# Column means of w1 in two halves, and a list that hands out PSUM's places

## The chip, the core and the metric

The kernel runs on one core of one Trainium2 chip. The metric is the device time of one execution in microseconds (us). The kernel before takes 205.06 us, the median of three runs (204.96 to 205.13). A core has a matrix engine (PE, whose weight loads are listed apart as PEld), a vector engine (DVE), an activation engine (ACT), a general engine (POOL) and a queue engine (SP) that mostly issues transfers. PE writes its results to PSUM, a small memory of eight banks; DVE and ACT read them from there. The large on-chip memory is SBUF.

## The reference, cut to what matters

One sequence of 2048 tokens with 512 channels goes through a long convolution and then through a two-layer network:

```
h  = x + LN(x) * (irfft(rfft(kv) * rfft(ssm_k)) + kv * ssm_D)   # kv = (short conv of k) * v
h2 = h + relu(LN(h) @ w1) @ w2                                   # w1: 512 x 1376, w2: 1376 x 512
```

The kernel does not apply the mean of the second normalisation to the tokens. Subtracting the mean of h over its 512 channels and then multiplying by w1 is the same as multiplying h by a w1 from whose every column its mean over the 512 rows has been taken. So the means of w1's 1376 columns are computed once, w1 is centered in place, and the scale of the normalisation is applied after the second product. The change concerns this piece of work: when the means are taken, and which PSUM tiles they lie in.

## The kernel before, in words

The program is written in one order by hand (a manual schedule): each engine carries out its instructions in the order in which the code emits them, and only waits for other engines where data or a buffer asks for it. Its stages are:

1. 0 to 48 us: tables, the short convolution, and the first stage of the transform of kernel and sequence (`stage1`).
2. 48 to 82 us: the product stage. Eight rounds of six units each (`pairs`, called u, and `sums`, called us). For each unit PE fills one PSUM tile (`u`, `us`), ACT copies one half of it to SBUF (`copy_k`, L449), and DVE multiplies the other half by that copy (`times`, L501). The u units write their products into `BK`, the us units into `BXs`, a part of the tile `BX`. The last units of the last round end with the products `=s1` (into `BXs`), `=u3` and `=u2` (into `BK`), in this order.
3. 82 to 83.5 us: the column means. POOL has added up the four row blocks of w1 in SBUF (`add_chunks`, into `wsum`, which lies in the tile `st`); four matmuls against a matrix of ones (L533, 344 columns each) add up the partitions. They go to two PSUM tiles, both named `pm`. ACT copies the second of them to SBUF (L633); DVE subtracts the means from w1 in four steps (`center`, L596), the first two from PSUM, the last two from the copy.
4. 83.5 to 106.8 us: the first inverse stage (`inv1`, L610), 16 blocks of four groups. Each group is one matmul of 256 columns that reads `BXs` and two of 128 columns that read `BK`. For the first two blocks the `BXs` matmuls are emitted ahead (`inv1_begin`), four for each block, and the `BK` matmuls follow. ACT or DVE copies each finished block to `ax`, two instructions a block (L278 on ACT, L280 on DVE). The last two blocks are cut into two and four tiles so that their copies end early.
5. 106.6 us: two matmuls of zeros (`fill`, L157) stand in PE's order while the last copies end.
6. 107.4 to 115.1 us: the second inverse stage for the first two of four token quarters (`inv2`, L701, 32 matmuls each). The first writes PSUM's upper four banks (`psZ0`), the second the lower four (`psZ`). After the first, DVE multiplies the result by the normalised x and adds x (`gate`, L687 and L688), which gives the input of the network for that quarter.
7. To the end: for each quarter the network's two layers (`mlp1` L713, `mlp2` L729), with the second inverse stage of the last two quarters and the gates in between.

PSUM's eight banks are one pool of four places of two banks each until the first inverse stage is over: `bank2` takes a tile from it, and the pool decides which place it gets. Before the last round's end every place has been used many times, so each new tile waits for the engine that read the former tile in the same place last. In the built program the column means' first tile lies in the place of the unit u1 of the last round, the second in that of s1; the first block of the inverse stage lies in that of u3, the second in that of u2, the third in that of the second means' tile (which ACT copies), the fourth in that of the first means' tile (which DVE reads in `center`).

Other work stands beside this: SP loads x for the first quarter after the product stage (`load_x`) and transposes it (`lift`), DVE takes the normalisation's statistics behind `center` (`ln1_stats`, then `ln1_norm` after block 3), and POOL prepares angles (`ec_turns`).

Of the kernel before, what the change touches and what calls it, by code (L numbers as in the profile page):

```python
# [9 lines left out]
ALU = mybir.AluOpType  # L10
BF16 = mybir.dt.bfloat16
F32 = mybir.dt.float32
F32R = mybir.dt.float32r
I32 = mybir.dt.int32
PSUM = bass.MemoryType.PSUM
P = 128
# [40 lines left out]
def kernel(  # L57
# [13 lines left out]
    nc = tc.nc  # L71
    _, S, D = A_q.shape
    DFF = B_w1.shape[1]
# [3 lines left out]
    DC = D // P  # L77
# [5 lines left out]
    pl = _Pools(tc)  # L83
# [6 lines left out]
    turnp = pl.push("turnp")  # L90
    early = pl.push("early", side="right")
    kp = pl.push("kp", side="right")
    psum = pl.push("psF", bufs=4, space=PSUM)

# [51 lines left out]
        nc.scalar.activation(out=out, in_=turns, func=ACT.Sin, scale=(-TURN if neg else TURN) / M,  # L148
                             bias=(pbias if neg else nbias)[:])

    def bank2(name):
        return psum.tile([P, 2, 512], F32, tag="ps", name=name)[:]

    def fill(ps, n):

        for _ in range(n):
            nc.tensor.matmul(out=ps, lhsT=zero[:], rhs=zero[:].unsqueeze(1).to_broadcast([P, 4, P]), start=True, stop=True, skip_group_check=True)  # L157
# [110 lines left out]
    def ec_wrap(q):  # L268
        nc.vector.tensor_single_scalar(out=ecw[q], in_=ecw[q], scalar=8191, op=ALU.bitwise_and)
# [85 lines left out]
    ones = consts.tile([P, P], F32R, name="ones")  # L355
# [66 lines left out]
    BXt = bxp.tile([P, 32, 66, DC * 2], F32R, tag="X", name="BX")  # L422
# [14 lines left out]
    wsum = stf[:, 0:DFF]  # L437
# [14 lines left out]

    def pairs(k1):

        ps = bank2("u")
        begun = []

        def do(what):
            x = "KX".index(what[0])
            for i in range(2):  # L460
                t = st[:, k1, 64:192] if i == 0 else st[:, k1, 0:128]
                for dp, pq in enumerate(halves):
                    nc.tensor.matmul(out=ps[:, dp, 256 * x:256 * x + 256], lhsT=t[pq], rhs=cols((BK, BX)[x], pq, k1, i),  # L463
                                     start=not begun, stop=(i == 1), tile_position=(64 * dp, 0), skip_group_check=True)
                begun.append(i)
        return do, ps, "ktu", BK[:, :, :, k1, :]

    def sums(k1):

        ps = bank2("us")  # L470
        begun = []
        ways = {}

        def do(what):
            x, way = "KX".index(what[0]), int(what[1])
            last = {}
            for i in range(2):
                for dp, pq in enumerate(halves):
                    k = k1 + (dp + way - 1) % 2
                    if i == 0 and dp == 0 and (3 - way, dp) in ways:  # L480

                        turn = nc.tensor.nop()
                        for d in range(2):
                            tc.add_manual_dep(turn.ins, ways[3 - way, d], mybir.DependencyInfo(mybir.DependencyClass.Sync, mybir.DependencyReason.DATA))
                    mm = nc.tensor.matmul(out=ps[:, k % 2, 256 * x:256 * x + 256], lhsT=smc[pq, k // 4 % 3, i, k % 4, :],  # L485
                                     rhs=cols((BK, BX)[x], pq, k, i), start=not begun, stop=(i == 1 and what in begun),
                                     tile_position=(64 * dp, 0), skip_group_check=True)
                    last[dp] = mm.ins.name
                begun.extend((what[0] + "12"[2 - way], i))
            for dp in range(2):  # L490
                ways[way, dp] = last[dp]
        return do, ps, "kts", BXs[:, :, k1:k1 + 2, :].rearrange("p g k x -> p k g x")
# [5 lines left out]
    def times(unit, kt=None):  # L498
        do, ps, tag, o = unit
        kt = copy_k(unit) if kt is None else kt  # L500
        nc.vector.tensor_tensor(out=o, in0=ps[:, :, 256:512].rearrange("p b (g x) -> p b g x", x=8),  # L501
                                in1=kt[:].rearrange("p b (g x) -> p b g x", x=8), op=ALU.mult)

# [2 lines left out]
    for c in range(8):  # L508
        units, early = {}, {}
        for step in (OTHER if c else FIRST).split():  # L510
# [6 lines left out]
            u = step[:2]  # L517
# [5 lines left out]
        if c in (2, 4, 5):  # L523
            add_chunks(max(c - 3, 0))

    FS = 344
    cen = {}

    def column_means(ns):
        ps = bank2("pm")  # L530
        for b, n in enumerate(ns):
            cen[n] = ps[:, b, 0:FS]
            nc.tensor.matmul(out=cen[n], lhsT=ones[:], rhs=wsum[:, n * FS:(n + 1) * FS], start=True, stop=True)  # L533
        return ps[:, :, 0:FS]

    column_means((0, 1))
    pm23 = column_means((2, 3))
    pl.pop("skp")
    pl.pop("stp")
    pl.pop("prod")  # L540
# [22 lines left out]
    qT = [late.tile([P, 4, DC, P], BF16, name="qT0")[:]] + [None] * 3  # L563
# [28 lines left out]
        rows_T(qT[q], src)  # L592

    def center(n):
        fs = slice(n * FS, (n + 1) * FS)
        nc.vector.tensor_tensor(out=w1[:, :, fs], in0=w1[:, :, fs],  # L596
                                in1=cen[n].unsqueeze(1).to_broadcast([P, DC, FS]), op=ALU.subtract)

    ax1 = late.tile([P, 32, 2, P], F32R, name="ax1")
    ax = (BX[:, 1].rearrange("p n k x -> p n (k x)").rearrange("p n (m c) -> p n m c", m=2), ax1[:])  # L600
# [28 lines left out]
                     blocks[b][:, 0:n].rearrange("p i d a n -> p a n (i d)")[:, rho].rearrange("p (n m) c -> p n m c", m=2))  # L629

    lift(0)
    later = qT[0].rearrange("p i r t -> p (i r t)").bitcast(F32)[:, 0:2 * FS].rearrange("p (n f) -> p n f", n=2)
    nc.scalar.copy(out=later, in_=pm23)  # L633
    cen[2], cen[3] = later[:, 0], later[:, 1]
    inv1_begin(0)
    inv1_begin(1)

# [3 lines left out]
    for b in range(16):  # L641
        inv1(b, "ADAD" if b == 15 else "AD" if b == 14 else "D" if b in (7, 9, 11, 13) else "A")
        if b == 0:
            for n in range(4):
                center(n)
            ec_wrap(1)
            ln1_stats(0)
        if b == 3:
            ln1_norm(0)
        if b in (8, 9, 10, 11):  # L650
            ec_sins(1, (b - 8,))
        if b == 11:
            load_x(1)
    fill(bank2("psz")[:, 0, :], 2)
    M = bkp.tile([P, 32768], BF16, tag="K", name="M")
    top = [0]

# [28 lines left out]
    def gate(q):  # L686
        nc.vector.tensor_tensor(out=flat(qT[q]), in0=pzs[q][:].rearrange("p i r a n -> p (i r a n)"), in1=flat(qT[q]), op=ALU.mult)  # L687
        nc.vector.tensor_tensor(out=flat(xT[q]), in0=flat(qT[q]), in1=flat(xT[q]), op=ALU.add)  # L688
        hT[q] = xT[q]
        nc.sync.dma_start_transpose(out=xh[q].rearrange("p i (r c) -> p (i r) c", r=DC),  # L690
                                    in_=hT[q].rearrange("p i r t -> p (i r) t"))

    def inv2(q, pool):
        pz = pool.tile([P, 4, DC, 4, 32], F32, tag="pz", name="pz")
        pzs[q] = pz
        for j in range(16):
            i, a = j // 4, j % 4
            w = min(2, 4 - a)
            n2 = 16 * a + 4 * q + i
            for rho in range(2):  # L700
                nc.tensor.matmul(out=pz[:, i, :, a:a + w, :].rearrange("p (s r) a n -> p s r (a n)", s=2),  # L701
                                 lhsT=ax[rho][:, n2 // 2, n2 % 2, :],
                                 rhs=ecore[q][:, rho, i, :, :, 32 * a:32 * a + 32 * w],
                                 start=(rho == 0), stop=(rho == 1), skip_group_check=True)
# [30 lines left out]
            if hook is not None:  # L735
                hook(i)

    pl.pop("psF")
    psz = pl.push("psZ", space=PSUM)
    psz0 = pl.push("psZ0", space=PSUM)  # L740
    ec_turns(2)
    inv2(0, psz0)
    gate(0)
    inv2(1, psz)
    pl.pop("psZ0")
# [68 lines left out]
```

## Time and profile before

| view | value |
|---|---|
| time, median of 3 runs | 205.06 us (204.96 to 205.13) |
| profiled execution: its own time | 205.23 us |
| its span, first to last instruction | 203.1 us |
| outside the span | 2.1 us |
| PE busy | 194.7 us, 96% of the span |
| DVE, ACT, POOL busy | 140.3, 115.1, 79.3 us |
| matmul `pm` (L533) | 4 of 344 columns, 0.32 to 0.43 us each, 82.43 to 83.52 us |
| `center` (L596) | 4 of 1.58 us, 83.99 to 90.07 us |
| copy of the second means (L633) | 0.74 us at 84.19 us |
| mean granted clock of PE | 0.997 |

A PE at 96% says that the chain of work runs through PE nearly everywhere, not that each of its instructions is as short as it could be: matmuls overlap, so the distance from one to the next (here mostly 0.12 us) is what counts, not the duration of one (0.28 us for 256 columns). Time is lost or won where PE stands still or where an instruction leaves PE's queue. Times below are microseconds from the start of the span.

### The profile page before, as it was taken

The numbers are of one execution on the slowest core, as the hardware profiler recorded it, in microseconds if no ns is written. First come the engines' busy times: TensorE is split into PE (matmuls) and PEld (weight loads), VectorE is DVE, ScalarE is ACT, GpSimd is POOL, SyncE is SP. The second block draws the span as 40 slices with busy tenths as digits, with TensorE's granted clock in tenths as the row PEclk, the third lists the DMA queues.
The fourth block names the chain that finished last, engine by engine and source line by source line (L and its number), as shares of the span: only waits on it lengthen the run. The fifth ranks groups of instructions, "written<-read, shape, count | busy, mean of one in ns | idle before, by whom it ended". The sixth has DMA issues, their size and how long they took to land.

```text
span 203.1 us, 4751 instructions
## 1 busy us (share of the span) xinstructions
PE 194.7 (96%) x1929; PEld 136.9 (67%) x1929; DVE 140.3 (69%) x252; ACT 115.1 (57%) x198; POOL 79.3 (39%) x127
## 2 busy tenths in 40 slices
PE   8899899999999999999999999999999999999991
PEld 2565556988899999899998744475445744444460
DVE  4999988796899989997561968994298560360130
ACT  4986785898688777685980188206930174036200
POOL 7979998960569994302003032062002200002000
PEclk9999999999999999999999999999999999999998
DMA  5999990003400000151736999999734705110011
GB/s 190 330 181 226 170 163 3 3 5 91 190 3 0 3 3 0 46 135 29 107 102 203 183 210 213 177 154 94 88 65 97 138 13 103 35 57 14 0 52 52
DMA packets 47300, 19.94 MB, mean 98 GB/s; under 512 B 42186, under 2 KB 45744, under 8 KB 47280
## 3 DMA queue, kind: packets, MB, share of 16 engines
q1 hardware_dynamic: 43616, 16.14, 41.9%
q10 hardware_dynamic: 3664, 3.51, 6.0%
q8 instruction: 15, 0.25, 0.6%
q14 instruction: 5, 0.04, 0.1%
HBM read 7.02 MB, written 2.10 MB: 45 GB/s over the span
## 4 chain that ended last, share of the span: by engine, by line
PE 73%; DVE 1%; ACT 0%; issue 0%
PE ps1m L713 19%; PE ps2m L729 19%; PE psi L610 11%; PE us L485 9%; PE pz L701 7%; PE u L463 7%; PE pm L533 1%; DVE BX L280 0%; DVE BX L501 0%; ACT kts L449 0%; DVE M L731 0%; DVE ax L280 0%
## 5 line engine op out<-in xcount | busy, mean ns | idle before, releaser
L715 ACT ACTIVATE M<-ps1m 128x512 bf16<-128x512 f32 (+1 forms) x44 | 25.1, 595 | 49.4 <-PE ps1m L713 39.0
L729 PE MATMUL ps2m<-M 128*128 128x512 bf16 (+3 forms) x187 | 38.7, 366 | 0.0
L729 PEld LDWEIGHTS <-M 128*128 128x128 bf16 (+1 forms) x187 | 18.2, 98 | 19.9
L713 PEld LDWEIGHTS <-w 128*128 128x128 bf16 (+1 forms) x176 | 17.4, 100 | 19.9
L572 POOL TENSOR_SCALAR rstd<-mv 128x4 f32<-128x4 f32 x8 | 2.2, 276 | 70.2 <-DVE mv L570 70.2
L409 POOL TENSOR_TENSOR smc<-st 64x256 fp32r<-64x256 f32 x32 | 22.8, 731 | 11.2 <-PE us L485 10.3
L731 DVE SCALAR_TENSOR_TENSOR M<-ps2m,rstd,M 128x512 bf16<-128x512 f32 (+1 forms) x13 | 9.2, 707 | 24.2 <-PE ps2m L729 15.7
L501 DVE TENSOR_TENSOR BK<-u,ktu 128x512 fp32r<-128x512 f32 x32 | 21.2, 685 | 3.8 <-ACT ktu L449 3.5
L610 PE MATMUL psi<-inv,BK 128*128 128x128 f32 x128 | 21.1, 255 | 0.0
L449 ACT COPY ktu<-u 128x512 f32<-128x512 f32 x32 | 18.1, 600 | 5.3 <-PE u L463 4.4
L610 PE MATMUL psi<-inv,BX 128*128 128x256 f32 x64 | 20.5, 338 | 0.0
L610 PEld LDWEIGHTS psi<-inv,BK 128*128 128x128 f32 x128 | 19.7, 197 | 0.0
L713 PE MATMUL ps1m<-M,w 128*128 128x512 bf16 (+1 forms) x88 | 19.3, 379 | 0.0
L713 PE MATMUL ps1m<-xT,w 128*128 128x512 bf16 (+1 forms) x88 | 19.3, 379 | 0.0
L485 PE MATMUL us<-BK,smc 64*128 64x256 f32 x128 | 14.4, 300 | 0.4 <-DVE BX L280 0.4
L463 PE MATMUL u<-BK,st 64*128 64x256 f32 x128 | 13.6, 290 | 0.3 <-DVE BX L501 0.2
L485 PE MATMUL us<-BX,smc 64*128 64x256 f32 x128 | 13.3, 281 | 0.0
L463 PE MATMUL u<-BX,st 64*128 64x256 f32 x128 | 13.1, 283 | 0.0
L278 ACT CAST BK<-ps 128x512 fp32r<-128x512 f32 x16 | 9.1, 587 | 6.4 <-PE ps L312 4.4
L610 PEld LDWEIGHTS psi<-inv,BX 128*128 128x128 f32 x64 | 12.1, 196 | 0.3 <-DVE BK L501 0.3
L568 DVE BATCH_NORM_STATS2 st<-M 128x6 f32<-128x512 bf16 x20 | 12.3, 677 | 0.0
L687 DVE TENSOR_TENSOR qT<-pz,qT 128x2048 bf16<-128x2048 f32 x2 | 4.6, 2290 | 10.6 <-DMA qT<-M 6.5
(132 smaller groups left out, 411.6 us busy)
## 6 DMA issues: line engine op xcount, KB each, us to landing
E<-in_A_ssm_k_dram SPq DMA_DIRECT2D x1, 2048.0 KB
out_dram<-M ACTq DMA_DIRECT2D x15, 128.0 KB
w<-in_B_w_dram SPq DMA_DIRECT2D x1, 1376.0 KB
M<-in_B_w_dram ACTq DMA_DIRECT2D x1, 1280.0 KB
M<-in_A_q_dram SPq DMA_DIRECT2D x8, 128.0 KB
xh<-in_A_q_dram SPq DMA_DIRECT2D x4, 128.0 KB
xr<-in_A_q_dram SPq DMA_DIRECT2D x4, 128.0 KB
out_dram<-M ACTq DMA_DIRECT2D x2, 64.0 KB
```

The source lines that it names most:

```text
L409: nc.gpsimd.tensor_tensor(out=smc[pq, c % 3, i, :, 64 * dp:64 * dp + 64], in0=st[pq, ks, 64:128].bitcast(F32), in1=st[pq, ks, 0:64].bitcas ...
L449: nc.scalar.copy(out=kt[:], in_=ps)
L463: nc.tensor.matmul(out=ps[:, dp, 256 * x:256 * x + 256], lhsT=t[pq], rhs=cols((BK, BX)[x], pq, k1, i), start=not begun, stop=(i == 1), til ...
L485: mm = nc.tensor.matmul(out=ps[:, k % 2, 256 * x:256 * x + 256], lhsT=smc[pq, k // 4 % 3, i, k % 4, :], rhs=cols((BK, BX)[x], pq, k, i), s ...
L501: nc.vector.tensor_tensor(out=o, in0=ps[:, :, 256:512].rearrange("p b (g x) -> p b g x", x=8), in1=kt[:].rearrange("p b (g x) -> p b g x", ...
L568: nc.vector.bn_stats(out=st[:, i, :], in_=src[:, i, :])
L610: nc.tensor.matmul(out=o if part == 0 else o[:, P * part - P:P * part], lhsT=src[:, g // 2, :, g % 2::2].rearrange("p c r -> p (c r)"), rh ...
L701: nc.tensor.matmul(out=pz[:, i, :, a:a + w, :].rearrange("p (s r) a n -> p s r (a n)", s=2), lhsT=ax[rho][:, n2 // 2, n2 % 2, :], rhs=ecor ...
L713: nc.tensor.matmul(out=ps1[:fsz, :].rearrange("p (i t) -> p i t", i=4), lhsT=w1[:, c, fc * P:fc * P + fsz], rhs=hT[sc][:, :, c, :], start= ...
L715: nc.scalar.activation(out=h1T[:fsz, fc, :], in_=ps1[:fsz, :], func=ACT.Relu)
L729: nc.tensor.matmul(out=ps2, lhsT=h1T[:ksz, fc, i * P:(i + 1) * P], rhs=w2[:ksz, fc, d0:d0 + w], start=(fc == 0), stop=(fc == NFC - 1))
L731: nc.vector.scalar_tensor_tensor(out=o[:, d0:d0 + w], in0=ps2, scalar=rstd2[:, t, :], in1=xh[sc][:, i, d0:d0 + w], op0=ALU.mult, op1=ALU.add)
```

## The change

The column means are split in three parts of 512, 352 and 512 columns (`THIRDS`) in place of four of 344. The first two are taken where all four were, into the two banks of one `pm` tile, and both are subtracted by DVE from PSUM after block 0. For the third part ACT copies the 512 sums, not the means, from `wsum` to two free columns (k = 32 and 33) of the tile `BX`; this copy replaces that of the second `pm` tile. Behind the first inverse stage one matmul takes the third part's means from there (512 columns in groups of 16, tile `pm2`), in place of one of the two matmuls of zeros. DVE subtracts them (`center(2)`) between `inv2(0)` and `gate(0)` in its order.

The pool of four places becomes four pools of one place, and `bank2` takes the first place of a list. A place goes to the list's end at once, except for the units of the product stage and for `pm`, which are put back when their last reader has been emitted (`leave`). `pm2` must lie in one of the two lower places, since `inv2(0)` writes the upper banks.

In the built program the places of all tiles up to the last product are, but for their numbers, those of before. Behind it, `pm` lies in the place of u1; the first block of the inverse stage in that of s1, the second in that of u3, the third in that of u2, the fourth in that of the first block, the fifth in that of the second, and the sixth in that of `pm`. So the first `BXs` matmul waits for the product `=s1`, the fifth for `=u3`, and the first `BK` matmul for `=u2`. The order on all engines is otherwise that of before.

```
-    psum = pl.push("psF", bufs=4, space=PSUM)
+    psum = [pl.push(f"psF{i}", bufs=1, space=PSUM) for i in range(4)]
+    places = list(range(4))
+    held = {}
...
-    def bank2(name):
-        return psum.tile([P, 2, 512], F32, tag="ps", name=name)[:]
+    def bank2(name, hold=False, at=None):
+        at = places[0] if at is None else at
+        places.remove(at)
+        ps = psum[at].tile([P, 2, 512], F32, tag="ps", name=name)[:]
+        if hold:
+            held[id(ps)] = at, ps
+        else:
+            places.append(at)
+        return ps
+
+    def leave(ps):
+        places.append(held.pop(id(ps))[0])
...
-        ps = bank2("u")
+        ps = bank2("u", True)
...
-        ps = bank2("us")
+        ps = bank2("us", True)
...
                                 in1=kt[:].rearrange("p b (g x) -> p b g x", x=8), op=ALU.mult)
+        leave(ps)
...
-    FS = 344
+    THIRDS = ((0, 512), (512, 864), (864, DFF))
     cen = {}
-    def column_means(ns):
-        ps = bank2("pm")
-        for b, n in enumerate(ns):
-            cen[n] = ps[:, b, 0:FS]
-            nc.tensor.matmul(out=cen[n], lhsT=ones[:], rhs=wsum[:, n * FS:(n + 1) * FS], start=True, stop=True)
-        return ps[:, :, 0:FS]
-
-    column_means((0, 1))
-    pm23 = column_means((2, 3))
+    def column_means(ps, n, sums):
+        cen[n] = ps[:, 0:THIRDS[n][1] - THIRDS[n][0]]
+        nc.tensor.matmul(out=cen[n] if n < 2 else cen[n].rearrange("p (g x) -> p g x", x=16), lhsT=ones[:], rhs=sums, start=True, stop=True)
+
+    pm = bank2("pm", True)
+    for n in range(2):
+        column_means(pm[:, n], n, wsum[:, slice(*THIRDS[n])])
+    wlast = BXt[:, :, 32:34, :].rearrange("p g k x -> p g (k x)")
+    nc.scalar.copy(out=wlast, in_=wsum[:, slice(*THIRDS[2])].bitcast(F32).rearrange("p (g x) -> p g x", x=16))
...
-        fs = slice(n * FS, (n + 1) * FS)
+        fs = slice(*THIRDS[n])
...
-    later = qT[0].rearrange("p i r t -> p (i r t)").bitcast(F32)[:, 0:2 * FS].rearrange("p (n f) -> p n f", n=2)
-    nc.scalar.copy(out=later, in_=pm23)
-    cen[2], cen[3] = later[:, 0], later[:, 1]
...
         if b == 0:
-            for n in range(4):
+            for n in range(2):
                 center(n)
+            leave(pm)
...
-    fill(bank2("psz")[:, 0, :], 2)
+    pm2 = bank2("pm2", at=[p for p in places if p < 2][0])
+    column_means(pm2[:, 0], 2, wlast)
+    fill(pm2[:, 1], 1)
...
-    pl.pop("psF")
+    for i in (3, 2, 1, 0):
+        pl.pop(f"psF{i}")
...
     inv2(0, psz0)
+    center(2)
     gate(0)
```

More of the change, by code (lines that the diff above doesn't have):

```diff
@@ L594, in center @@
     def center(n):
-        fs = slice(n * FS, (n + 1) * FS)
+        fs = slice(*THIRDS[n])
         nc.vector.tensor_tensor(out=w1[:, :, fs], in0=w1[:, :, fs],
-                                in1=cen[n].unsqueeze(1).to_broadcast([P, DC, FS]), op=ALU.subtract)
+                                in1=cen[n].unsqueeze(1).to_broadcast([P, DC, fs.stop - fs.start]), op=ALU.subtract)
     ax1 = late.tile([P, 32, 2, P], F32R, name="ax1")
```

## The prediction

> **What bounds the kernel now.** I read the busy shares first, then the chain of waits in order of time, then the waits of PE, and last the timeline of the two places that the change touches. The page gives PE as the bound, and its chain holds no long wait:
>
> ```profile
> PE 194.7 (96%) x1929; PEld 136.9 (67%) x1929; DVE 140.3 (69%) x252; ACT 115.1 (57%) x198; POOL 79.3 (39%) x127
> ...
> PE 73%; DVE 1%; ACT 0%; issue 0%
> ```
>
> The chain in order of time (start, length, what) shows the two joints, 82.48 to 83.53 and 106.76 to 107.42. What PE saves there moves everything behind it, unless another wait holds it back:
>
> ```profile
> 82.48 1.04 PE pm L533 x4
> 83.52 0.01 issue
> 83.53 23.22 PE psi L610 x192
> 106.76 0.02 issue
> 106.78 0.29 DVE BX L280
> 107.07 0.21 DVE ax L280
> 107.28 0.14 issue
> 107.42 7.65 PE pz L701 x64
> 115.06 0.01 issue
> 115.07 9.66 PE ps1m L713 x44
> ```
>
> The timeline of the first joint (start, length, engine, line, what, in brackets the idle time and its releaser) shows that the joint is not only PE's work:
>
> ```profile
> 82.20 0.68 DVE L501 TENSOR_TENSOR BX<-us,kts 128x512 fp32r<-128x512 f32 x1
> ...
> 82.80 1.28 DVE L501 TENSOR_TENSOR BK<-u,ktu 128x512 fp32r<-128x512 f32 x2
> ...
> 82.94 0.30 PEld L533 LDWEIGHTS pm<-st,ones 128*128 128x128 f32 x2 [0.23 <-DVE BX L501]
> 83.53 1.16 PEld L610 LDWEIGHTS psi<-inv,BX 128*128 128x128 f32 x8 [0.30 <-DVE BK L501]
> ...
> 84.61 1.97 PEld L610 LDWEIGHTS psi<-inv,BK 128*128 128x128 f32 x16
> ```
>
> DVE's last three products end at 82.88, 83.48 and 84.08. PE's queue starts three times right behind them: the second pair of means at 82.94 (0.06 later; its place is that of s1), the first block of the inverse stage at 83.53 (place of u3), the second block at 84.13 (place of u2). A finer look at the weight loads shows the last:
>
> ```profile
> 83.89 0.20 PEld L610 LDWEIGHTS psi<-inv,BX 128*128 128x128 f32 x1
> ...
> 84.13 0.19 PEld L610 LDWEIGHTS psi<-inv,BX 128*128 128x128 f32 x1
> ```
>
> The loads follow each other by 0.12, but between the fourth (83.89) and the fifth (84.13) lie 0.24. So PE follows DVE here, and behind DVE's end at 84.08 stand the second block's four BX matmuls (84.13 to 84.61) before the first BK matmul at 84.61. The inverse stage then runs without a wait.
>
> The second joint and what follows:
>
> ```profile
> 106.58 0.61 PE L157 MATMUL psz<-zero 128*128 128x512 bf16 x2
> ...
> 106.99 0.28 DVE L280 CAST ax<-psi 128x128 fp32r<-128x128 f32 x1
> ```
>
> PE is idle here but for zeros: it waits for the copy that ends at 107.27 and loads weights again at 107.38. Of the 0.80 from 106.58 to 107.38 the zeros take two distances of 0.23 (106.58, 106.81).
>
> **The first joint, step by step.** Before: means until 82.94 (first pair), a wait, second pair, a wait until 83.53, four BX, a wait until 84.13, four BX, BK at 84.61. After, with the same DVE products (nothing ahead of them moves, as the places up to there are the same):
> - Two means matmuls from 82.41, as now: their place is u1's, free now as then. The two first of now were 0.24 apart (82.43, 82.67); the 864 columns at 0.24 to 0.26 for 344 take 0.60 to 0.65, at most until 83.06.
> - The first block waits for 82.88 (s1's product) and starts at 82.94 to 83.06; four BX at 0.12 end at 83.42 to 83.54.
> - The second block waits for 83.48 (u3's place): 83.53; four BX until 84.01.
> - The first BK matmul waits for the last product, 84.08: 84.13, not 84.61.
>
> So the gain is 84.61 − 84.13 = **0.48 us**, the four BX matmuls that now stand behind the last product. Of the 512 columns fewer (0.36 to 0.39) nothing adds to it: the wait for DVE is the end of the path either way. No less than 0.42 either, if the renewed start costs another 0.06.
>
> A price for the new wait: queued behind that BK matmul is the whole inverse stage, and it starts at 84.13 in any case, when the old order started the second block.
>
> **Places in the inverse stage.** Only three places turn at first. The fourth block waits for ACT's two copies of the first block: these end at 86.88 now, the fourth block starts at 87.93 (block 3 begins at 86.50, each takes 1.43), so 1.05 are left, and both move by 0.48. The fifth has 87.87 against 89.36. The sixth waits for DVE's `center(1)`: centering costs 1.58 for 344 columns, so 2.35 and 1.62 for 512 and 352, from 83.99 to 87.96; the block starts at 90.8 − 0.5 = 90.3. All three hidden; without that cover each would cost its lateness.
>
> **ACT's copy of sums.** 128x512 from SBUF, not in the trace. From below 0.59 (a cast of 128x512), from above 0.74 (128x688, the copy that it replaces); I take 0.6. It starts at 83.11, behind ACT's last copy, and ends at 83.7; ACT's next work is block 1's cast at 85.81 − 0.48. Hidden by 1.6. What waits for it (POOL's `mhalf`, SP's load of x) starts at 84.22 now, behind DVE's 84.08, and stays there. SP's later transfers follow the copies and gates and move with them; DVE's statistics come 2.1 earlier (87.96 for 90.07), as x has landed by 88.40, when SP transposes it; none is on the path.
>
> **The second joint.** `pm2` replaces one zero matmul (0.23). 512 columns of this type are not in the trace: from below 0.24 (two of `inv2`'s 256 columns at 0.12), from above 0.63 (the longest means matmul, 0.425, by 512/344). I take 0.39, the 0.26 between means matmuls by 512/344, being the same operands. With the zero matmul 0.62 of 0.80: hidden, 0.18 to spare; at the upper end 0.86, so 0.06 late.
>
> **Center(2).** 2.35 on DVE from its last copy (106.79 after the shift) or `pm2`'s end, at most until 109.3. DVE then waits: now it is idle for 4.15 until `gate(0)` at 111.42, 110.94 after the shift. `inv2(1)`, which waits for `center(2)`, loads weights at 111.10 now, 110.62 then. 1.3 to spare. If the cover were gone it would count fully: `mlp1(0)` loads weights at 115.04, just 0.07 behind the gate's end (113.74 + 1.23), so a late gate moves the path at once.
>
> POOL's angles (106.82 to 109.02) run beside it. The `center` steps that ran beside such angles (84.28 to 86.48) took 1.577 and 1.581, those without 1.583 and 1.587, so I charge nothing. [...]
>
> **Sum.** 0 − 0.48 + 0 + 0 = −0.48 (bounds −0.48 and −0.36, with 0.06 from a renewed start and 0.06 from `pm2`). The profiled execution: 205.23 − 0.48 = 204.75, span 202.6. It stands 0.17 above the median, so against 205.06 the time is **204.58 us**. About 0.2%, 0.41 us, is what a measurement of this kernel can tell from no change, and the gain is near that.
>
> **Rivals.**
> [...]
> - *The gain is given back.* The earlier stage meets something that doesn't move, a transfer or ACT's copies, and waits. **205.06**, within 0.2%. For it: `mlp1(0)` already follows DVE's gate by 0.07. Against: that gate is released by PE (idle 4.15, released by `pz`), and every issue behind 84 us is too.
> - *Slower: center(2) holds gate(0).* Its place is ahead of the gate in DVE's order. It decides from 110.94 on: it must take over 4.1, not 2.35, to delay the gate, and over 5.0 to make the kernel slower by 0.2% (0.48 + 0.41 more). Twice its price plus 0.4 for a late start, 5.1, would give 110.94 + 1.0 for the gate, so **205.6**. Against it: all four steps lie between 1.577 and 1.587.
> - *The list does not change the wait.* If the first block still had u3's place, the four BX would stay behind the last product: 0, **205.06**. The built order excludes this, and it goes with the second rival.
>
> **How the numbers follow.** Forecast 0.76 (its own range 204.35 to 204.75: 0.48, less up to 0.12, with 0.1 for the spread of runs and as much again for a joint that closes tighter); late joint 0.06; given back 0.11; slower 0.07. The predicted time is the forecast's, 204.58. Four fifths of the forecast lie beyond 0.41, so faster 0.61; the rest with the second and third case makes within 0.2% 0.32; slower 0.07. The range reaches from 204.3 to 205.1, over the late joint and the gain given back; outside stay the slower case and little else.
>
> **What would show it.** In the profile after: weight loads of `psi` at about 82.95, 83.53, and the first BK at 84.13, with DVE's last product still ending at 84.08; `pm` of two matmuls; block casts on ACT 0.48 earlier, with ACT still waiting for PE; `pm2` starting at about 106.1 and the first `pz` load at 106.9, still released by a copy; `center(2)` of 2.35 ending before 109.4, with DVE idle ahead of the gate; PE without a wait from there on; a span of 202.6. The prediction is wrong if the first BK load is not at 84.13, if `pz` is released by PE itself, or if the gate starts without DVE idle ahead of it.

## The result, and the profile after

The changed kernel takes 204.27 us (median of 8 runs, 203.94 to 204.74), the kernel before 205.13 us beside it (8 runs, 204.91 to 205.31). The ratio is 0.9955, with a 95% interval of 0.9937 to 0.9974: it is faster by 0.45%. The forecast was 204.58 us and a gain of 0.48; the gain is 0.86 us, and the time lies 0.03 us below the range.

The profiled execution of the changed kernel took 204.07 us, with a span of 202.3. The page gives nearly the same shares by engine as before:

```profile
PE 73%; DVE 1%; issue 0%; ACT 0%
```

The chain of waits of the changed kernel (start, length, what) around the two joints:

```profile
82.23 0.59 PE pm L547 x2
82.81 23.18 PE psi L626 x192
...
106.01 0.29 DVE BX L293
106.31 0.21 DVE ax L293
106.51 0.14 issue
106.65 7.64 PE pz L717 x64
```

Of the 1.04 us of means 0.59 are left, and the inverse stage follows them without a gap. From its start on the chain has the lengths of before: 23.18 (23.22), the same wait for the last copy, 7.64 (7.65). The timeline of the first joint (start, length, engine, line, what, idle time and releaser) shows what became of the three starts behind VectorE's (DVE's) products:

```profile
82.18 0.63 PE L547 MATMUL pm<-st,ones 128*128 128x512 f32 x2
82.55 1.28 DVE L514 TENSOR_TENSOR BK<-u,ktu 128x512 fp32r<-128x512 f32 x2
82.69 1.15 PEld L626 LDWEIGHTS psi<-inv,BX 128*128 128x128 f32 x8 [0.23 <-DVE BX L514]
...
83.88 1.26 PEld L626 LDWEIGHTS psi<-inv,BK 128*128 128x128 f32 x10
```

DVE's last product ends at 82.55 + 1.28 = 83.83, and the first weight load from `BK` stands at 83.88: 0.05 behind it. Before, it was 84.61 against 84.08, so 0.53. All eight `BX` matmuls now lie in front. Everything in this profile stands 0.25 us earlier than in that of before, since the work ahead of it ended earlier in this execution (more of that under "The head"); distances within a profile don't depend on that.

The timeline of the second joint:

```profile
105.81 0.44 PE L547 MATMUL pm<-BX,ones 128*128 128x512 f32 x1
...
106.10 0.39 PE L170 MATMUL pm<-zero 128*128 128x512 bf16 x1
106.22 0.28 DVE L293 CAST ax<-psi 128x128 fp32r<-128x128 f32 x1
106.52 2.29 DVE L612 TENSOR_TENSOR w<-w,pm 128x2048 bf16<-128x2048 bf16 x1
106.62 0.19 PEld L717 LDWEIGHTS pz<-core,BX 128*128 128x128 f32 x1 [0.43 <-issue]
...
110.65 2.29 DVE L703 TENSOR_TENSOR qT<-pz,qT 128x2048 bf16<-128x2048 f32 x1 [1.84 <-PE pz L717]
```

The means matmul is 0.29 ahead of the matmul of zeros, the next weight load still follows the copy that ends at 106.50, and `center(2)` leaves DVE idle for 1.84 us ahead of `gate(0)`.

Where the time went is seen when each run's time is divided into its span and what lies outside it. The table has medians; its row for the kernel before is the 29 runs taken beside the first four experiments:

| kernel | runs | time | span | outside the span |
|---|---|---|---|---|
| before | 29 | 205.15 | 203.0 | 2.20 (2.11 to 2.25) |
| changed | 8 | 204.27 | 202.5 | 1.83 (1.76 to 1.84) |
| changed, again | 12 | 204.31 | 202.5 | 1.83 (1.77 to 1.85) |

The span fell by 0.5, which is the forecast's 0.48. Another 0.37 went from outside the span, which the prediction had carried over unchanged. The two ranges outside the span, 2.11 to 2.25 and 1.76 to 1.85, don't overlap.

### The profile page after: what moved, and what is told of

Same layout as the page of the kernel before. It is cut to its first block, busy times and chain, and to the rows that moved or that the text cites. A ratio compares the mean times of both kernels' runs of the same rounds, so it can differ in the third digit from the quotient of the medians.

```text
span 202.3 us, 4740 instructions
## 1 busy us (share of the span) xinstructions
PE 194.9 (96%) x1919; PEld 137.0 (68%) x1927; DVE 140.5 (69%) x251; ACT 114.9 (57%) x198; POOL 79.5 (39%) x127
## 4 chain that ended last, share of the span: by engine, by line
PE 73%; DVE 1%; issue 0%; ACT 0%
PE ps1m L729 19%; PE ps2m L745 19%; PE psi L626 11%; PE us L498 9%; PE pz L717 7%; PE u L476 7%; DVE BX L293 0%; DVE BX L514 0%; ACT kts L462 0%; PE pm L547 0%; DVE M L747 0%; DVE ax L293 0%
## 5 line engine op out<-in xcount | busy, mean ns | idle before, releaser
L514 DVE TENSOR_TENSOR BX<-us,kts 128x512 fp32r<-128x512 f32 x16 | 11.0, 686 | 0.8 <-ACT kts L462 0.5
```

## The experiments

The expectations, which are quoted as they were written before each run, call DVE VectorE, ACT ScalarE and POOL GpSimd.

### Both kernels again, the list alone, and no list

The first two are the two kernels as they are. The third takes from the change only the list, with `hold` for both `pm` tiles; the four means of 344 columns stay as before. The fourth takes everything but the list: one pool of four places as before, and `center(2)` ahead of that pool's end.

```
# the list alone
-        ps = bank2("pm")
+        ps = bank2("pm", True)
+        pms.append(ps)
...
+    leave(pms[1])          # behind ACT's copy of the second pair
...
+                if n == 1:
+                    leave(pms[0])   # behind center(1)
# no list (against the changed kernel)
-    for i in (3, 2, 1, 0):
-        pl.pop(f"psF{i}")
+    center(2)
+    pl.pop("psF")
...
-    center(2)
```

> The kernel before, against itself. Theory A (the joint ahead of the first inverse stage gives 0.48 us; what the measured gain of 0.86 has beyond it lies in the head of the kernel or outside the span and changes from execution to execution): ratio 1.000, within 0.002; in the profile the first BK weight load of the inverse stage stands again 0.53 us behind the end of DVE's last product, but the time of that product may differ by up to 0.3 us from 84.08, with the angle step of DVE at about 20 us (L269, 1.16 us in the first profile of before, 0.89 in that of after) somewhere between 0.7 and 1.2. Theory B (the head is faster in the changed kernel because its places are numbered otherwise): L269 again 1.16 and the last product again at 84.08.

> The changed kernel again. Theory A: about 204.6, a gain between 0.4 and 0.9 us with five rounds; the first BK weight load 0.05 us behind the end of DVE's last product, and that product anywhere between 83.8 and 84.1. Theory B: 204.27, the last product again at 83.83 and L269 again at 0.89.

> The list of places alone, with four means of 344 columns in two tiles as before. Theory A: same as before, 205.1, ratio within 0.002 of 1, since the places up to the last product are those of before but for their numbers and the joint is that of before (first BK load 0.53 us behind the last product). Theory B: the list alone gives what the joint does not, so 204.75 (0.38 faster) with the joint as before.

> The moved means alone, in one pool of four places as before; center(2) then stands ahead of the pool's end, so the second inverse stage waits for it. Theory A: the joint gives its 0.48 without the list (the first BK load 0.05 us behind the last product), and the second joint loses the 2.3 us of center(2), as pz starts behind it: 205.1 - 0.48 + 2.3 = 206.9. Theory B: the same loss, without the gain of the head: 207.2. If the list were what opens the first joint, the first BK load would be 0.53 us behind and the time 207.4.

| kernel | time (runs) | ratio to before | span | outside | first `BK` load behind DVE's last product |
|---|---|---|---|---|---|
| before again | 205.11 (12) | 1.0002 (0.9986 to 1.0017) | 202.9 | 2.20 | 0.53 |
| changed again | 204.31 (12) | 0.9957 (0.9941 to 0.9972) | 202.5 | 1.83 | 0.06 |
| list alone | 205.02 (12) | 0.9985 (0.9971 to 0.9999) | 202.85 | 2.17 | 0.54 |
| no list | 208.53 (6) | 1.0156 (1.0119 to 1.0194) | 206.35 | 2.17 | 0.06 |

Two things follow. The first joint (the wait ahead of the first inverse stage) closes without the list too (0.06), and the list alone doesn't close it (0.54): there the four means still fill two tiles, and the second of these takes the place that the first block has in the changed kernel. It is the single `pm` tile that lets the first two blocks move up, and the list isn't needed for that. And only the changed kernel has 1.83 outside the span; its parts alone have not.

Of the two theories, B falls. The list alone numbers its places as the changed kernel does, yet its last product ends at 84.15, as late as before (84.08, and 84.14 when run again), and it takes 205.02 us, not 204.75. Theory A was right in that the rest of the gain lies outside the span, and wrong in that it changes from execution to execution: the changed kernel run again has 1.83 there once more. The angle step took 1.16 us again in the kernel before, and 0.70, not 0.89, in the changed one.

The list is needed at the second joint. In the kernel without it PE waits there for `center(2)`, since the old pool ends behind that step. The windows of its timeline (start and end, length, busy time of PE, PEld, DVE, ACT, POOL with their counts, PE's granted clock, the transfers' share and GB/s) show more than the wait:

```profile
107.00:109.00 2.00, 0.00 (x0) 0.00 (x0) 1.98 (x1) 0.00 (x0) 1.33 (x2) 1.00 0.59 167
109.00:111.00 2.00, 1.88 (x12) 1.91 (x13) 0.00 (x0) 0.00 (x0) 0.00 (x0) 0.78 0.99 325
111.00:113.00 2.00, 2.00 (x11) 2.00 (x11) 0.00 (x0) 0.00 (x0) 0.00 (x0) 0.50 1.14 278
```

PE waited for 2.47 us, and about a microsecond after it went on its clock was halved. The first two products of the second inverse stage took 9.21 us in place of 7.64, as the chain of waits has it:

```profile
109.12 9.21 PE pz L703 x64
```

That is why the loss in the span was 3.4 and not the 1.8 that was expected (2.3 for `center(2)`, less 0.48).

### Is it the idle time that halves the clock?

The kernel without the list, with nine more matmuls of zeros in the wait:

```
     fill(pm2[:, 1], 1)
+    fill(bank2("psz")[:, 0, :], 9)
```

> The kernel without the list (center(2) ahead of the change of pools), with nine zero matmuls more on PE in the 2.47 us in which it waits for center(2). Without them the granted clock fell to 0.50 between 111 and 113 us and the second inverse stage's first two products took 9.21 us in place of 7.65. If the idle time itself lowers the clock: clock 1.00 throughout, span 206.35 less 1.56, 204.8, and with 2.17 outside (VectorE 319 instructions) about 207.0 us. Rival (the clock falls for another reason, the load of the stage or of the kernel): clock and time as without them, 208.5 us.

Measured: 207.19 us (4 runs; ratio 1.0117, 1.0096 to 1.0138), span 205.0, outside 2.20. The chain of waits of its profile gives the second inverse stage its old length, though PE still starts it behind `center(2)`, which ends at 108.58:

```profile
108.72 7.64 PE pz L704 x64
```

The granted clock is 1.00 in every window from 105 to 117 us; the longest time in which PE had no matmul is 0.53. So in this kernel the fall goes with the idle time: it comes behind 2.47 us of it and not behind 0.53. The medians differ by 1.34 us; the runs are few and spread (206.49 to 208.20 with the zeros, 206.72 to 209.56 without), but the mean granted clock separates them: 0.998 to 1.000 in all four with the zeros, 0.981 to 0.991 in five of the six without.

By the windows (0.78 from 109 to 111, 0.50 from 111 to 113, 0.87 from 113 to 115) the clock of the kernel without the list stood at 0.50 from about 110.1 to 113.5 us. In that stretch most `pz` matmuls of 256 columns follow each other by 0.21 to 0.22, ahead of it and behind it mostly by 0.12. One of the six runs without the zeros had a clock of 0.996 and a span of 204.5; why, no profile shows. Nor does this wait account for every lower clock: two of the twelve runs of the kernel before again have a mean of 0.989, and no wait of PE in its profile is longer than 1.0 us.

### What lies outside the span: one instruction more

In the built programs the kernels differ in how many instructions each engine has, waits that stand alone included. DVE has 319 before, in the list alone and without the list, and 320 in the changed kernel: one `center` fewer, but 64 waits that stand alone in place of 62. (The traces list two fewer for each kernel, 317 and 318, with the same 62 and 64 waits.) The other engines' counts don't go with the time outside. So one instruction was added to DVE at the start, a memset of 128 elements:

```
     nc.vector.memset(pbias[:], 0.5 * TURN)
+    nc.vector.memset(pbias[:], 0.5 * TURN)
```

> The kernel before with one VectorE instruction more: the memset of pbias (128 elements, at the start) stands twice, so VectorE has 320 instructions, as the changed kernel has, in place of 319. The time outside the span (device time less span) has been 2.2 us in the kernel before and in the list alone, 2.17 without the list, 1.83 in the changed kernel. Theory A (the last fetch of instructions after the span depends on where VectorE's stream of instructions ends): outside 1.83, span 203.0 as before, so about 204.8 us, 0.35 below the kernel before. Rival (it is something else in the changed kernel, its places or its order at the end): outside 2.2, about 205.15 us.

> The changed kernel with the same memset twice: VectorE has 321 instructions. Theory A as a threshold (320 or more): outside 1.83, about 204.3 us. Theory A as an exact place (320 alone): outside 2.2, span 202.5, about 204.7 us. Rival (something else in the changed kernel): outside 1.83, 204.3 us.

The kernel before with one memset more took **204.75 us** (10 runs; ratio 0.9971, 0.9951 to 0.9991), span 202.95, outside **1.82**. It does more work and is 0.4 us faster, nearly all of it outside the span (0.38): theory A's numbers, and the rival is out. The changed kernel with 321 instructions took 204.41 (6 runs), outside 1.94, so neither of the two expected values; the step is not a plain threshold.

The traces have two instruction queues; in the span of the kernel before and of the changed one q8 has 15 fetches of 16384 bytes each and q14 five of 8192. The second shows a last fetch behind the last instruction: 1.61 us behind it in the kernel before (at 204.68, the last instruction ends at 203.07), 1.33 with the memset, 1.15 in the changed kernel (1.43 when run again). That this fetch is where the 0.37 go isn't shown: 1.15 and 1.43 belong to the same time outside the span (1.81 and 1.82 in these two executions), and with 321 instructions the fetch stands at 1.11 while the time outside is 1.94. Which engine this fetch serves the trace doesn't say.

Two more kernels bear on it.

### The third means left out, and the same with one instruction more

```
     pm2 = bank2("pm2", at=[p for p in places if p < 2][0])
-    column_means(pm2[:, 0], 2, wlast)
-    fill(pm2[:, 1], 1)
+    fill(pm2[:, 1], 2)
...
-    center(2)
     gate(0)
```

> The changed kernel without the third part of the means: its matmul is replaced by a second zero matmul in the same place, and the subtraction from columns 864 to 1375 is left out (these columns stay uncentred). VectorE has 319 instructions. If the second joint hides the third means, as the prediction has it, the span stays at 202.5 us; if it holds up PE there, the span falls by 0.1 to 0.3. Theory A: outside 2.2, so about 204.7 us. Rival: outside 1.83, 204.3 us or below.

> The kernel without the third part of the means (columns 864 to 1375 stay uncentred, its matmul replaced by a zero matmul), with one memset twice at the start, so that VectorE has 320 instructions in place of 319 and gate(0)'s first product is its 194th instruction in place of its 193rd, the first behind 192 (three times 64). Without the memset gate(0) began 0.72 us behind the start of the last matmul that it needs, in place of 0.37 in every other kernel, and the time was 205.0. Theory A (VectorE's instructions are fetched in pieces of 64, and one that begins a piece is late): 0.37 again, span 202.5, outside 1.83, about 204.3 us, 0.7 below the kernel without the memset. Rival (the subtraction that is left out is what makes gate(0) late): 0.72, span 202.85, outside 1.83 at best, about 204.7 us.

Without the third means 205.01 us (10 runs; ratio 0.9998, 0.9989 to 1.0008): less work and 0.7 us more time than the changed kernel. Outside 2.17, as 319 instructions ask for. But the span was 202.85 too, where at most 202.5 was expected. The distance from the first `BK` load to the first `pz` load is 22.73 against 22.74, so leaving out the third means gains nothing at the second joint. The loss is at `gate(0)`. Its product may start when the first 32 matmuls of `pz` are done; the timeline of this kernel has the last of them and the gate:

```profile
110.42 0.28 PE L716 MATMUL pz<-core,ax 128*128 128x128 f32 x1
...
111.14 2.29 DVE L702 TENSOR_TENSOR qT<-pz,qT 128x2048 bf16<-128x2048 f32 x1 [4.50 <-PE pz L716]
```

0.72 us from one to the other, though DVE had been idle for 4.50 us. It is 0.37 in the changed kernel (110.28, 110.65), and before (111.05, 111.42). PE's next layer starts 0.37 us later for it: 8.02 us behind the first `pz` matmul (106.78, 114.80), in place of 7.65 before (107.42, 115.07). In this kernel the product is DVE's 193rd instruction, the first behind 192; in the others it is the 194th or 195th, and the 193rd is a wait that DVE reaches long before (2.2 us or more). (The counts are those of the built program; the trace lists one fewer up to here.) With the memset, which moves it by one, the timeline reads:

```profile
110.40 0.28 PE L717 MATMUL pz<-core,ax 128*128 128x128 f32 x1
...
110.77 2.29 DVE L703 TENSOR_TENSOR qT<-pz,qT 128x2048 bf16<-128x2048 f32 x1 [4.14 <-PE pz L717]
```

0.37 again, span 202.5, outside 1.81, time 204.33 us (10 runs; ratio 0.9962, 0.9941 to 0.9984): 0.68 less than without the memset. Both numbers came as theory A had them: the subtraction that is left out plays no part, the place in the stream of instructions does. What was shown is the effect of the place. In both traces the wait just ahead of the product ends at the same time (110.74 without the memset, 110.72 with it); the product then starts 0.40 us behind it in the one and 0.05 in the other. So DVE had all that it waited for, and the product itself started late. Why is open. Theory A's pieces of 64 are a guess that no run shows: the trace of the late kernel has no instruction fetch between 110.0 and 114.4 us, so none while the product was late.

### Is it the places that close the first joint?

The changed kernel, with the place that was left first kept back while the first two blocks take theirs; they get the places of u3 and u2, as before the change, with the columns split as after it.

```
     lift(0)
+    first = places.pop(0)
     inv1_begin(0)
     inv1_begin(1)
+    places.insert(0, first)
```

> The changed kernel, but the place that was left first (the last sums tile's) is kept back while the first two inverse blocks take theirs, so these get the places of the last two pair tiles, the second of them that of VectorE's last product. The columns are split as in the changed kernel. The prediction's theory (the gain at the first joint comes from the places that the first two blocks get): the first weight load from BK is issued 0.53 us behind the end of VectorE's last product again, in place of 0.05; span up by 0.48. At the end the last block then lies in a lower place, which was worth 0.18 in the list alone: net 0.3 more than the changed kernel, span 202.8, about 204.65 us with 1.83 outside. Rival (the gain comes from 512 columns fewer ahead of the first stage): the load stays within 0.1 us of the product, span 202.3, about 204.15 us.

The timeline of the first joint of this kernel:

```profile
82.80 1.28 DVE L514 TENSOR_TENSOR BK<-u,ktu 128x512 fp32r<-128x512 f32 x2
...
83.53 1.15 PEld L626 LDWEIGHTS psi<-inv,BX 128*128 128x128 f32 x8 [0.84 <-DVE BK L514]
...
84.61 0.79 PEld L626 LDWEIGHTS psi<-inv,BK 128*128 128x128 f32 x6
```

The first `BK` load is 0.53 behind the product again (84.08, 84.61). Its weight loads stand still for 0.84 us with 512 columns fewer ahead of them, so the fewer columns alone bring nothing at this joint: the gain is the places'. Span 202.8 as expected. The time is 204.94 us (10 runs; ratio 0.9986, 0.9966 to 1.0007) and not 204.65, since the time outside is 2.19. That was a miss of the expectation, not of theory A: with other places DVE needs one separate wait less (63 for 64 in the trace), 319 instructions in all.

Over the fifteen kernels run in this study the time outside follows DVE's count alone: 319 instructions in six kernels, 2.17 to 2.20; 320 in eight, 1.81 to 1.84; 321 in one, 1.94. (In the traces the three counts are 317, 318 and 319.) A memset alone moved a kernel from the first group to the second; what the count does to the time outside is not shown.

### How much time the second joint and `center(2)` have

The matmul of the third means three times in a row; and, in another kernel, `center(2)` followed by a subtraction of the same size into an unused part of `M`.

```
-    column_means(pm2[:, 0], 2, wlast)
+    for _ in range(3):
+        column_means(pm2[:, 0], 2, wlast)
...
     center(2)
+    nc.vector.tensor_tensor(out=h1b[1][:, 0:DC, :], in0=w1[:, :, 864:DFF],
+                            in1=cen[2].unsqueeze(1).to_broadcast([P, DC, 512]), op=ALU.subtract)
```

> The changed kernel with the matmul of the third means issued three times in a row into the same place, with the same sums. Two more at the pitch of 0.29 us seen in the changed kernel are 0.58 us. If the second joint has 0.30 us to spare there (PE goes on at 106.65, and its last zero matmul would let it go on from about 106.35), the first weight load of the second inverse stage comes 0.3 us later behind the first load from BK (23.0 us in place of 22.74), the span is 202.8 and the time about 204.6 us (320 VectorE instructions, 1.83 outside). Rival (the joint has no time to spare): 0.58 later, about 204.9. Rival (it has 0.6 or more): no change, 204.3.

> The changed kernel with a second subtraction of the same size as center(2) behind it on VectorE, written into a part of M that is not yet in use. In the changed kernel gate(0) starts 1.84 us behind center(2). The second subtraction takes 2.29 us, so gate(0) should start 0.45 to 0.5 us later; what follows it on PE was ready within 0.1 us of gate(0)'s second product, so the span grows by 0.4 to 0.5 us, to 202.95, about 204.8 us with 1.83 outside. Rival (gate(0) has time to spare of its own): no change, 204.3 us.

Three means matmuls: 204.38 us (10 runs; ratio 0.9966, 0.9948 to 0.9985), span 202.55, and 22.73 us from the first `BK` load to the first `pz` load against 22.74. No loss: the rival with at least 0.6 to spare. The chain now runs through PE:

```profile
105.81 0.75 PE pm L547 x3
...
106.79 7.41 PE pz L718 x64
```

0.25 each, and the next load is issued right behind the zeros, still 0.12 behind the last copy as in the changed kernel (106.33, 106.45). So the joint held two more matmuls, and PE has no time left there.

The second subtraction: 205.02 us (10 runs; ratio 0.9997, 0.9978 to 1.0016), span 203.2, which is 0.7 more and not 0.45. The timeline shows who was held:

```profile
110.25 0.27 PE L717 MATMUL pz<-core,ax 128*128 128x128 f32 x1
111.25 0.35 PE L717 MATMUL pz<-BX 128*128 128x256 f32 x1 [0.73 <-DVE M L761]
```

`inv2(1)` writes to the place in which `pm2` lies, so PE must wait until the last reader of `pm2` is done: 111.25, where without the wait 0.11 after 110.25 was due, 0.89 later. `gate(0)` was only 0.4 late. The cover of `center(2)` ends with `inv2(1)`, as the prediction said when it gave it 1.3 us, and not with the gate, as this experiment's expectation had it: in the changed kernel `inv2(1)` loads its first weights at 110.33 and `center(2)` ends at 108.81, so 1.5 us are to spare.

### The place of the last tile

In the list alone the first `pz` load came 22.57 us behind the first `BK` load (84.69, 107.26), in place of 22.77 before (84.61, 107.38), and there the last inverse tile lay in a lower place. `inv2(0)` writes the two upper ones. Two tries at having that in the changed kernel, each with one memset twice for 320 instructions: the last two tiles exchanged, and the exchange made at block 10, from which on the list's own order leads there.

```
# last two tiles exchanged (inv1 hands its argument to bank2 as at=)
-        inv1(b, "ADAD" if b == 15 ...)
+        inv1(b, "ADAD" if b == 15 ..., (None, None, 2, 1) if b == 15 else (None,) * 4)
# at block 10
+        inv1(b, "ADAD" if b == 15 ..., 2 if b == 10 else None)
```

> The changed kernel with the last two inverse tiles exchanged in their places: the third tile of the last block in place 2, the fourth in place 1, so that the places of the second inverse stage's first product (2 and 3) are empty before the last tile's second copy; and one memset twice at the start, which keeps VectorE at 320 instructions (it would have 319). The list alone gained 0.18 us where its last tile lay in a lower place. Expected: the first matmul of the second inverse stage waits for the first copy of the last tile and not for the second, 0.15 to 0.2 us earlier; span 202.3, outside 1.83, about 204.1 us. Rival (the third tile now waits for its place): the gain is lost in the last block, 204.3 us.

> The changed kernel, but the tenth inverse block takes place 2 (left by a VectorE block) where the list would give it place 1; from there on the list gives the order 0, 3, 2, 1, so that the last tile lies in place 1 and no tile of the last block takes a place before its turn. VectorE has 320 instructions (one memset stands twice). Expected: the last block as in the changed kernel, and the first weight load of the second inverse stage behind the last tile's first copy and not its second: 22.55 us behind the first load from BK in place of 22.74; span 202.3, outside 1.83, about 204.1 us. Rival (the copies of the last tile but one, on ScalarE, end no earlier): 22.74, 204.3 us.

The first try: 204.49 us (12 runs; ratio 0.9971, 0.9949 to 0.9993), span 202.65. `pz` did follow the last tile's first copy, but the third tile had to wait for its place (its matmuls start at 106.16, 0.23 us idle, released by DVE's copy of the former tile there), the last tile came later, and the distance from the first `BK` load to the first `pz` load grew from 22.74 to 22.90: the rival, and a little more than the gain lost.

At block 10: **204.18 us** (6 runs; ratio 0.9961, 0.9948 to 0.9974), span 202.35. The distance is 22.57 (84.57, 107.14); 22.55 was expected. The chain no longer has a wait at the second joint:

```profile
99.86 6.84 PE psi L627 x57
106.70 0.28 PE pm L548
106.97 0.23 PE pm L171
107.21 7.63 PE pz L718 x64
```

So the 0.2 of the list alone are the last tile's place, as the distance shows; in the time the difference to the changed kernel (0.09 to 0.13) lies within the spread of runs, so it isn't shown there.

### The head

In the first 50 us the kernels' profiles differ, in steps that the change doesn't touch: the last transposes of this part start between 33.78 and 34.73 us. One suspect was a mask of angles on DVE beside POOL's taps: 1.16 us before, 0.89 after, and 0.69 where the same step runs alone later. The kernel with the exchanged place, with that mask and the four sines behind it one group later:

```
-        if gb == 1:
+        if gb == 2:
             ec_wrap(0)
-        if gb in (2, 3, 4, 5):
-            ec_sins(0, (gb - 2,))
+        if gb in (3, 4, 5, 6):
+            ec_sins(0, (gb - 3,))
```

> The same, and in the first 50 us the mask of the first angles on VectorE and the four sines behind it are issued one group later, where GpSimd's taps no longer run beside it. The mask took 0.68 to 1.16 us in the kernels so far, and 0.69 alone; the kernels in which it took 0.68 to 0.89 reached the last transposes of the head 0.2 to 0.3 us earlier in three of five. If the mask sets that time: the transposes start at 34.0 in every profile and the median is 0.1 to 0.2 us below the kernel with the exchanged place alone, about 204.0 us. Rival (the head's spread comes from elsewhere): the same median within 0.1 us.

Measured: 204.09 us (5 runs, 203.89 to 204.35; ratio 0.9950, 0.9938 to 0.9962), 0.09 below the kernel without the move. The mask took 0.68 in both, yet the last transposes of the head start at 34.08 here and at 34.70 there. So the mask is not what sets them, and the head's spread stays open. This kernel has the lowest median of the study, 0.2 us below the changed one, but the intervals of the two ratios overlap, so that it is faster isn't shown.

## Why the prediction was wrong

**What failed.** The step "Sum", which takes 0.48 off the profiled execution's 205.23 and so carries the 2.1 us outside the span over unchanged. Its four terms (0, 0.48, 0 and 0) all lie within the span; that what lies outside can move is a term that it puts at nothing without a reason. The span moved as forecast: 0.48 forecast, 0.5 measured, 202.6 against 202.5 (median). The time outside fell from 2.20 to 1.83, as the change leaves DVE with 320 instructions in place of 319: the kernel before with one instruction more, which does nothing useful, has 1.82. Why the count matters stays open. Forecast and this term together, 0.48 + 0.37 = 0.85, are the measured 0.86. Nothing in the profile of before shows it. The count itself could have been taken from the built order; what it is worth only the experiment told.

**The first joint.** Right in mechanism and size. The load was to follow the last product by 0.05 and does (0.05, again 0.06). That the 512 columns fewer bring nothing by themselves was right: with the places of before and the new split, PE just waits longer. The prediction credited the list with the new places, as the name of one rival shows; the runs credit the single `pm` tile, which closes the joint without the list (0.06) while the list without it doesn't (0.54).

**The means' two matmuls and ACT's copy.** 0.60 to 0.65 against 0.63, and 0.6 against 0.63, both beside DVE's products as said. The 0.06 for a renewed start, held as a bound, was not paid.

**Places in the inverse stage.** Hidden as said: 22.74 us from the first `BK` load to the first `pz` load, 22.77 before.

**The second joint.** Hidden, with more to spare than the 0.18 forecast. The matmul of the means took 0.25 to 0.29 and not 0.39, and the load behind the zeros needs no 0.23 of its own: in the kernel with three means matmuls it is issued 0.05 behind the start of the zeros. The late joint among the chances stood for 0.96 us for this one matmul. No run shows such a length; the runs have 0.25 to 0.29, and two further matmuls cost nothing.

**`center(2)`.** 2.29 against 2.35, with 1.5 us to spare ahead of `inv2(1)` (1.3 forecast) and 1.84 ahead of `gate(0)`. The slower rival priced the gate and not the matmul that waits for `pm2`'s place. In the kernel with two subtractions that wait held PE: 0.7 us for 2.29.

**POOL beside it.** Nothing charged, nothing paid: 2.29 beside POOL's angles, and 2.29 for the second subtraction, which started after POOL had ended (108.23, 108.82). A subtraction with both inputs from SBUF beside POOL stands in no run here.

**The gain is given back.** It was not: from the first `pz` matmul to the start of DVE's last step it is 91.29 us before and 91.30 after.

## What to carry to other kernels

Make a forecast for the span and for what lies outside it separately, and compare both with the result: a change of a few tenths can lie in either, and one instruction more or less on one engine was worth 0.37 us outside the span and 0.35 inside it, nearly as much each as the change's own idea. When a matrix engine must wait for a buffer, look first at which tile the buffer was handed to, and at the last buffer of a stage as well as at the first: both joints here were set by the place of one tile. PE's wait of 2.47 us cost more than its length, as the clock fell to 0.50 behind it and the next 64 matmuls took 9.21 us in place of 7.64; matmuls of zeros in the wait took 1.3 us off the median.

## What the runs showed of the hardware

- The time outside the span went with DVE's number of instructions: 2.17 to 2.20 us with 319, 1.81 to 1.84 with 320, 1.94 with 321, in the fifteen kernels run.
- A DVE instruction in the place just behind 192 others started 0.72 us behind the start of the last matmul that it needed, in place of 0.37, after 4.5 us of idle time, with no instruction fetch in the trace at that time.
- PE's granted clock fell to 0.50 about one microsecond after a wait of 2.47 us (109.12, about 110.1) and stayed there until about 113.5, by windows of 0.78, 0.50 and 0.87; with 0.53 of idle time in its place it stayed at 1.00.
- A matmul of 512 columns in this 4-byte form takes 0.25 to 0.29 us from one to the next, against 0.23 for the bf16 zeros.
